# More squared tiles, an earlier norm chain and paired subtractions in a fused cross-covariance attention and highway layer

## The chip, the cores and the metric

The kernel runs on one NeuronCore of a Trainium2 chip. The metric is the time of one execution on the device, in microseconds. The engines are TensorE (PE, with its weight loads PEld), VectorE (DVE), ScalarE (ACT), GpSimd (POOL), and SyncE (SP), which only issues DMAs here.

## The reference

For each of four batches, q, k and v are 6336 x 256. The attention matrix is 256 x 256, a softmax over a product of columns that are normalized along the 6336 rows. Its output, all batches stacked to 25344 x 256, goes through a highway layer.

```python
qn = q / (np.linalg.norm(q, axis=1, keepdims=True) + 1e-06)
kn = k / (np.linalg.norm(k, axis=1, keepdims=True) + 1e-06)
s = kn.transpose(0, 2, 1) @ qn / tau
a = softmax(s)                       # along the last axis
x = (v @ a).reshape(B * S, D)
H = np.maximum(x @ w_h, 0.0)
T = 1.0 / (1.0 + np.exp(-(x @ w_t + b_t)))
out = T * H + (1.0 - T) * x
```

## The kernel before

The rows of a batch are 49 tiles of 128 and a last one of 64. Loads come from GpSimd's queue and turn f32 into f16. Two kinds of work run on PE.

*Scores.* For each tile, `emit_score` (L193) makes S += k^T q (two matmuls of 256 columns, L205) and the Gram blocks whose diagonals are the squared norms: two matmuls of 128 columns for k (L208), two for q (L214). For some runs of four tiles, the q Gram is replaced: ACT squares the tiles (L398), POOL adds halves (L404), DVE reduces the rest and the running sum into the next run's area (L411), and at the end two small f32 matmuls against ones (L457, "sums") add the column sums to the Gram. `decide` chooses such runs while it plans; there are 28 of them, none in batch 0.

*Slots.* Two tiles of v make a slot; there are 100, 25 in a batch. In each, PE transposes v (L236, "vtps"), DVE or ACT copies it out (L250, "vts"), and PE multiplies it by three 256 x 256 matrices that stand side by side in `mr`: a, a w_h and a w_t (L260, results x, h and zbank, four matmuls of 256 columns each). ACT fills zbank with the bias (L304) and makes T = sigmoid (tt, L301). DVE makes th = max(h, 0) T (L309) and ux = (T - 1) x (L317); POOL subtracts them, one slot at a time, into an out tile (L335), and SP stores four slots at once (L352). Two slots of zbank and four of th and ux are kept, seven out tiles (ORING), and three or more banks of PSUM for h and x.

*The chain.* Between the scores of a batch and its first slot stands `make_chain`. It takes the norms from the Gram diagonals (junk, L449; q first, then k), the root (ACT in batch 0, POOL's pow after, L475), adds 1e-6 and takes the reciprocal (L484, L490). The inverse norms of q are spread over all partitions by a matmul of a constant matrix with two diagonal matrices (dcat L494, cq L503). Then S is copied out (ssb, L464), multiplied by cq (L508), exponentiated (L519, in SBUF, with the inverse norms of k as scale), normalized into `mr` (L530, L533), transposed (at, L544; at_sb, L555) and multiplied by the highway's weights (ah, L563; copied at L574). Each of ACT's functions sqrt, exp and sigmoid needs another table, loaded at L435 or L519.

*The order.* A planner at the end of the kernel simulates the engines with given durations, and emits instructions in the order in which it would start them. Each engine has queues with a fixed order inside (chain, slots, transposes, scores on PE), and `step_pe`, `step_act`, `step_dve`, `step_pool` and `step_sp` say which one goes first. `slot_of_score` and S_END spread the scores of the next batch over the slots of this one, so that the chain of the next batch runs while slots of this one go on. Every engine then runs its list strictly in order. Stores are held back while loads queue; a held one is tied to the last subtraction that POOL had been given.

Of the kernel before, what the change touches and what calls it, by code (L numbers as in the profile page):

```python
# [60 lines left out]
def kernel(  # L61
# [38 lines left out]
    SQR, SQ_LATE = 4, 3  # L100
    CLOSE = 44
    DVE_SUBS, ACT_COPIES = 2, 77
    QRING, VRING, ORING = 4, 3, 7
    TTR, THR, VTR = 4, 4, 6
    OG = 4
    LASTS = list(range(16)) + [NPAIR - 1] + list(range(16, NPAIR - 1))
    PAIRS = [list(range(NPAIR))] * (B - 1) + [LASTS]
    S_END = [19, 44, 69]
# [15 lines left out]

    def nrows(i):
        return [P, REM] if i == NPAIR - 1 else [P, P]
# [6 lines left out]
    MM = lambda n: n / 2400.0 + 0.0025  # L133
# [59 lines left out]
    def emit_score(b, j):  # L193
        if j == 0:
            tags = ("S", "G") if b == 0 else ("hx1", "hx2")
            S_t[b] = psum_pool.tile([P, 2, C], f32, tag=tags[0], name=f"S{b}")
            G_t[b] = psum_pool.tile([P, 4, P], f32, tag=tags[1], name=f"G{b}")
        nr = REM if j == NS else P
        kk, qq = tile_of("k", b, j), tile_of("q", b, j)
        S, G = S_t[b], G_t[b]  # L200
        first, last = j == 0, j == NS
        gram_q = (b, j) not in squares
        for c in range(2):
            kc = kk[0:nr, bass.ts(c, P)]
            nc.tensor.matmul(  # L205
                S[:, c, :], kc, qq[0:nr, :], start=first and c == 0, stop=last and c == 1
            )
            nc.tensor.matmul(  # L208
                G[:, c, :], kc, kc, start=first and c == 0,
                stop=False, skip_group_check=True,  # L210
            )
        for c in range(2 if gram_q else 0):
            qc = qq[0:nr, bass.ts(c, P)]
            nc.tensor.matmul(  # L214
                G[:, 2 + c, :], qc, qc, start=False, stop=last and c == 1, skip_group_check=True
            )

    score = {}

    def make_score(b, j):  # L220
        t = Task(("S", b, j), "PE", 2 * MM(C) + 4 * MM(P), lambda e: emit_score(b, j))
        score[b, j] = t
        return t
# [67 lines left out]
    tts, ths, uxs, o_t, outs = {}, {}, {}, {}, {}  # L291
# [14 lines left out]
    def emit_th(t):  # L306
        ths[t] = work_pool.tile([P, 2, C], f32, tag="th", bufs=THR, name=f"th{t}")
        for pr, us in parts_of(t):
            nc.vector.scalar_tensor_tensor(  # L309
                out=ths[t][pr, us, :], in0=hx["h", t][pr, us, :], scalar=0.0,  # L310
                in1=tts[t][pr, us, :], op0=AluOp.max, op1=AluOp.mult,
            )

    def emit_ux(t):
        uxs[t] = work_pool.tile([P, 2, C], f32, tag="ux", bufs=THR, name=f"ux{t}")
        for pr, us in parts_of(t):
            nc.vector.scalar_tensor_tensor(  # L317
                out=uxs[t][pr, us, :], in0=tts[t][pr, us, :], scalar=1.0,
                in1=hx["x", t][pr, us, :], op0=AluOp.subtract, op1=AluOp.mult,
# [10 lines left out]
    def emit_sub(t, e):  # L330
        ot, o0 = out_tile(t)
        outs[t] = (ot, o0)
        sub = nc.vector if e == "DVE" else nc.gpsimd
        for pr, us in parts_of(t):
            ins = sub.tensor_tensor(  # L335
                out=ot[pr, o0 + us.start : o0 + us.stop, :], in0=ths[t][pr, us, :],
                in1=uxs[t][pr, us, :], op=AluOp.subtract,
# [25 lines left out]
    squares = set()  # L363
    runs = []
    areas = []
# [3 lines left out]
    def decide(b, j, now):  # L369
        if b == 0 or j == NS:  # L370
            return
        g = group_of(QG[b], j)
        g0, ns = QG[b][g]
        if j == CLOSE:
            mine = [r for r in runs if r.name[1] == b]
            if mine:
                chains[b]["sums"].after.append((mine[-1], TO_PE))
                sums_t[b] = len(runs) % SQR
        if g > 0 and j < CLOSE and (j - g0) % CH == 0 and g0 + ns - j >= CH:
            if sum(1 for r in runs if r.end is None) < SQ_LATE:  # L380
                squares.update((b, jj) for jj in range(j, j + CH))
                make_run(b, g, j)

    def make_run(b, g, j):
        n = len(runs)
        first = n == 0 or runs[-1].name[1] != b
        half = 1 if first else 2

        def area(m):
            if m % SQR == len(areas):  # L390
                areas.append(
                    work_pool.tile([P, CH + 1, C], f32, tag=f"sq{m}", bufs=1, name=f"sq{m}")
                )
            return areas[m % SQR]

        def square(e):
            o = j - QG[b][g][0]
            nc.scalar.activation(  # L398
                out=area(n)[:, 1:, :], in_=tiles["q", b, g][:, o : o + CH, :], func=Act.Square
# [17 lines left out]
        sq = Task(("sq", b, j), "ACT", 0.2 + CH * C / 1200.0, square)  # L417
        ad = Task(("add", b, j), "POOL", 0.1 + half * C * 0.00235, halves, [(sq, LAG)])
        rd = Task(("red", b, j), "DVE", 1.0, reduce, [(ad, LAG)])
        sq.after.append((task_of_load["q", b, g], LAND))  # L420
        if n >= SQR:
            sq.after.append((runs[n - SQR], LAG))
        if n >= 1:
            rd.after.append((runs[n - 1], LAG))
        runs.append(rd)
        if ("q", b, g) in recycler:
            recycler["q", b, g].after.append((sq, LAG + 0.2))
# [9 lines left out]
    def make_chain(b):  # L437
        st = {}
        T = {}
        last = score[b, NS]  # L440

# [13 lines left out]
        def pe_sums(e):  # L455
            for c in range(2 if b in sums_t else 0):
                nc.tensor.matmul(  # L457
                    G_t[b][:, 2 + c, :], areas[sums_t[b]][:, 0, bass.ts(c, P)], ones32,
                    start=False, stop=True, skip_group_check=True,
                )  # L460
# [5 lines left out]
        def root(kind):  # L466
            def emit(e):
                if "nrm" not in st:
                    st["nrm"] = work_pool.tile([P, 4], f32, tag="nrm", name=f"nrm{b}")
                o = 2 if kind == "q" else 0  # L470
                dst, src = st["nrm"][:, o : o + 2], st["n2"][:, o : o + 2]
# [8 lines left out]
        def invs(kind):  # L480
            def emit(e):
                o = 2 if kind == "q" else 0
                nrm = st["nrm"][:, o : o + 2]
                nc.vector.tensor_scalar(  # L484
                    out=nrm, in0=nrm, scalar1=1e-6, scalar2=None,
                    op0=AluOp.add, op1=AluOp.bypass,
                )
                if "inv" not in st:
                    st["inv"] = work_pool.tile([P, 4], f32, tag="inv", name=f"inv{b}")
                nc.vector.reciprocal(out=st["inv"][:, o : o + 2], in_=nrm)  # L490
                if kind == "q":
                    dcat = work_pool.tile([P, 2, P], f32, tag="dcat", bufs=1, name=f"dcat{b}")
                    for c in range(2):
                        nc.vector.tensor_scalar(  # L494
                            out=dcat[:, c, :], in0=ident0, scalar1=st["inv"][:, 2 + c : 3 + c],
                            scalar2=None, op0=AluOp.mult, op1=AluOp.bypass,
                        )
                    st["dcat"] = dcat
            return emit

        def pe_cq(e):
            cq = bank_tile(T["cq"], f"cq{b}")
            nc.tensor.matmul(cq[:, 0, :], taus, st["dcat"][:, :, :], start=True, stop=True)  # L503
# [10 lines left out]
        def exps(c):  # L514
            def emit(e):
                if c == 0:
                    st["rs"] = work_pool.tile([P, 2], f32, tag="rs", name=f"rs{b}")
                ar = st["ssb"]
                nc.scalar.activation(  # L519
                    out=ar[:, c, :], in_=ar[:, c, :], func=Act.Exp,  # L520
# [4 lines left out]
        def softmax(c):  # L525
            def emit(e):
                if c == 0:
# [6 lines left out]
                    out=mr_t[b][:, c, 0:C], in0=st["ssb"][:, c, :],  # L534
# [49 lines left out]
        after = [(last, PE_LAG)]  # L584
        if b > 0:
            add("sums", "PE", 0.5, pe_sums, [(score[b, CLOSE], 0.0)])
# [503 lines left out]
```

## Time and profile before

| | |
|---|---|
| median of 20 runs | 274.66 us (274.38 to 277.28) |
| the profiled execution, its own time | 274.74 us |
| its span, first to last instruction | 272.6 us |
| PE, DVE, ACT, POOL busy | 250.1, 207.1, 176.4, 203.7 us |
| matmuls | 2632 |
| TensorE clock granted | 0.996 of full |
| HBM read, written | 78.38, 25.95 MB |

Busy times are unions over the span. A matmul's duration in the trace contains its pipeline's latency; what counts for PE's pace is the distance of the starts. A row of the windows names a stretch of the span and the busy time of each engine in it, with the count of instructions in brackets.

### The profile page before, as it was taken

What the parts mean: (1) busy time and instruction counts of PE and PEld (TensorE: products, weight loads), DVE (VectorE), ACT (ScalarE), POOL (GpSimd) and SP (SyncE); (2) the same over time, 40 slices, a digit from 0 to 9 for tenths busy, and PEclk for the clock granted to TensorE, in tenths of its full rate; (3) what the DMA queues carried; (4) which work ended last, traced back from release to release, by engine and by line L of the source; (5) the groups of instructions that cost most, each with busy time, mean ns of one, the idle gap of its engine ahead of it and who ended that gap; (6) DMA issues with size and microseconds to landing.
All of it is one profiled execution on the core that took longest, in us unless ns stands there. A gap on an engine that the chain in (4) does not pass through costs nothing.

```text
span 272.6 us, 6603 instructions
## 1 busy us (share of the span) xinstructions
PE 250.1 (92%) x2632; PEld 217.4 (80%) x2632; DVE 207.1 (76%) x423; ACT 176.4 (65%) x292; POOL 203.7 (75%) x216
## 2 busy tenths in 40 slices
PE   0996897899999999999999999999999979999990
PEld 0686786788999886899999886999999847998780
DVE  2000036949989798899899798899999799999883
ACT  3310037858675478877575577968785788898880
POOL 5133463879999855998999857899998557988780
PEclk9999999999999999999999999999999999999998
DMA  7999999999999999999999999999999999793434
GB/s 211 213 215 213 204 204 222 214 209 217 216 208 214 219 213 291 250 299 288 275 299 243 219 227 284 264 299 297 271 258 253 353 408 266 173 338 159 185 126 182
DMA packets 16143, 66.08 MB, mean 242 GB/s; under 512 B 1777, under 2 KB 4338, under 8 KB 13170
## 3 DMA queue, kind: packets, MB, share of 16 engines
q0 software_dynamic: 11040, 38.67, 71.4%
q1 hardware_dynamic: 4786, 26.22, 24.3%
q10 hardware_dynamic: 288, 0.79, 0.7%
q8 instruction: 20, 0.33, 0.5%
q14 instruction: 9, 0.07, 0.1%
HBM read 78.38 MB, written 25.95 MB: 383 GB/s over the span
## 4 chain that ended last, share of the span: by engine, by line
PE 74%; DMA 12%; DVE 9%; issue 1%; POOL 1%; ACT 0%; DVEq 0%
PE zbank L260 14%; PE x L260 14%; PE h L260 14%; PE S L205 13%; DMA k<-in_k_dram 10%; PE vtps L236 7%; PE G L208 7%; PE G L214 2%; DVE th L309 2%; DMA qk<-in_k_dram 2%; DVE ux L317 2%; DVE mr L533 1%; DVE vts L250 1%; DVE nrm L484 1%; PE ah L563 1%
## 5 line engine op out<-in xcount | busy, mean ns | idle before, releaser
L335 POOL TENSOR_TENSOR o<-th,ux 128x512 f32<-128x512 f32 x94 | 120.3, 1292 | 24.5 <-DVE ux L317 22.8
L260 PEld LDWEIGHTS <-vts 128*128 128x128 f16 (+1 forms) x1200 | 111.2, 98 | 18.2 <-issue 6.2
L205 PE MATMUL S<-q,k 128*128 128x256 f16 x392 | 81.6, 278 | 10.6 <-ACT k L763 6.4
L301 ACT ACTIVATE tt<-zbank 128x512 f32<-128x512 f32 x100 | 59.7, 597 | 45.2 <-PE zbank L260 23.3
L309 DVE SCALAR_TENSOR_TENSOR th<-h,tt 128x512 f32<-128x512 f32 (+1 forms) x104 | 68.6, 663 | 12.0 <-ACT tt L301 9.0
L208 PE MATMUL G<-k 128*128 128x128 f16 x392 | 73.8, 222 | 0.0
L317 DVE SCALAR_TENSOR_TENSOR ux<-tt,x 128x512 f32<-128x512 f32 (+1 forms) x104 | 67.8, 655 | 0.0
L260 PE MATMUL x<-mr,vts 128*128 128x256 f16 (+1 forms) x400 | 60.5, 273 | 0.7 <-DVE th L309 0.7
L260 PE MATMUL zbank<-mr,vts 128*128 128x256 f16 (+1 forms) x400 | 60.5, 273 | 0.0
L260 PE MATMUL h<-mr,vts 128*128 128x256 f16 (+1 forms) x400 | 60.5, 273 | 0.0
L304 ACT COPY zbank<-btb 128x512 f32<-128x512 f32 x98 | 57.8, 591 | 2.9
L205 PEld LDWEIGHTS <-k 128*128 128x128 f16 x392 | 39.0, 100 | 15.9 <-ACT k L763 6.4
L208 PEld LDWEIGHTS <-k 128*128 128x128 f16 x392 | 39.1, 100 | 1.2 <-issue 0.3
L236 PE MATMUL vtps<-ident,v 128*128 128x128 f16 x392 | 38.2, 219 | 1.7 <-DVE vts L250 1.4
L250 DVE COPY vts<-vtps 128x512 f16<-128x512 f16 x82 | 34.3, 418 | 6.4 <-PE vtps L236 5.4
L404 POOL TENSOR_TENSOR sq<-sq 128x512 f32<-128x512 f32 (+1 forms) x28 | 33.9, 1213 | 3.2 <-ACT sq L398 3.2
L236 PEld LDWEIGHTS <-v 128*128 128x128 f16 x392 | 28.0, 98 | 5.0 <-issue 2.8
L155 POOL DMA_DIRECT2D q<-in_q_dram x25 | 14.0, 561 | 23.9 <-PE G L214 21.3
L449 DVE SCALAR_TENSOR_TENSOR junk<-G,ident 128x128 f32<-128x128 f32 x16 | 4.7, 291 | 33.5 <-PE G L214 33.1
L411 DVE TENSOR_REDUCE sq<-sq 128x256 f32<-128x768 f32 x28 | 28.7, 1026 | 1.6 <-POOL sq L404 1.6
L398 ACT ACTIVATE sq<-q 128x1024 f32<-128x1024 f16 x28 | 29.2, 1054 | 0.0
L214 PE MATMUL G<-q 128*128 128x128 f16 x168 | 24.0, 226 | 0.0
(67 smaller groups left out, 143.1 us busy)
## 6 DMA issues: line engine op xcount, KB each, us to landing
out_dram<-o SPq DMA_DIRECT2D x23, 1024.0 KB, 8.9
v<-in_v_dram POOLq DMA_DIRECT2D x11, 768.0 KB, 17.9
q<-in_q_dram POOLq DMA_DIRECT2D x7, 768.0 KB, 18.8
k<-in_k_dram POOLq DMA_DIRECT2D x7, 768.0 KB, 20.8
q<-in_q_dram POOLq DMA_DIRECT2D x9, 512.0 KB, 13.5
k<-in_k_dram POOLq DMA_DIRECT2D x9, 512.0 KB, 14.6
v<-in_v_dram POOLq DMA_DIRECT2D x4, 832.0 KB, 19.2
q<-in_q_dram POOLq DMA_DIRECT2D x4, 256.0 KB, 12.8
```

The lines of the kernel that those rows point to most:

```text
L205: nc.tensor.matmul(S[:, c, :], kc, qq[0:nr, :], start=first and c == 0, stop=last and c == 1)
L208: nc.tensor.matmul(G[:, c, :], kc, kc, start=first and c == 0, stop=False, skip_group_check=True,)
L214: nc.tensor.matmul(G[:, 2 + c, :], qc, qc, start=False, stop=last and c == 1, skip_group_check=True)
L236: nc.tensor.transpose(ps[:, u, c, 0:r], vt[0:r, bass.ts(c, P)], ident[0:r, 0:r])
L250: cp(out=sb, in_=ps)
L260: nc.tensor.matmul(dst[0:r, u, :], vT_t[t][:, u, kt, 0:r], mr[:, kt, off : off + C], start=(not seeded and kt == 0 and (u == 0 or i == NPA ...
L301: nc.scalar.activation(out=tts[t], in_=zbank[t % 2], func=Act.Sigmoid)
L304: nc.scalar.copy(out=zbank[t % 2], in_=btb)
L309: nc.vector.scalar_tensor_tensor(out=ths[t][pr, us, :], in0=hx["h", t][pr, us, :], scalar=0.0, in1=tts[t][pr, us, :], op0=AluOp.max, op1=A ...
L317: nc.vector.scalar_tensor_tensor(out=uxs[t][pr, us, :], in0=tts[t][pr, us, :], scalar=1.0, in1=hx["x", t][pr, us, :], op0=AluOp.subtract, ...
L335: ins = sub.tensor_tensor(out=ot[pr, o0 + us.start : o0 + us.stop, :], in0=ths[t][pr, us, :], in1=uxs[t][pr, us, :], op=AluOp.subtract,)
L404: nc.gpsimd.tensor_tensor(out=sq[:, 1 : 1 + half, :], in0=sq[:, 1 : 1 + half, :], in1=sq[:, 1 + CH - half : 1 + CH, :], op=AluOp.add,)
```

## The change

- The runs of squared tiles are a fixed list (RUNS): 22 of q and 17 of k in batches 1 to 3, 39 in all. Each kind has areas of its own, four for q and two for k.
- The last tiles of each batch (TAIL: 6, 12, 10, 7) are taken apart: all their q Grams, then their k Grams, then their S. The 64-row tile goes ahead of them. The norms wait only for the Grams.
- The subtraction is done in place: th is written into the out tile and ux subtracted from it, for two slots in one instruction of 128 x 1024. The last eight slots are done singly, the subtraction of slot 97 is split between POOL and DVE.
- 1e-6 is not added: a constant column of the tile nrm holds it, and a reduction over two columns adds it to the root. cq is made by two matmuls, each with the inverse norm repeated over 128 columns as weights and the identity over tau as moving operand; dcat is gone.
- Exp writes to PSUM where a bank is to be had (both halves in batches 0 and 3, the first half in batches 1 and 2). Its table is loaded ahead by an instruction of its own, and no sigmoid is planned between it and the load of the sigmoid table.
- 28 copies of vts at fixed slots go to ACT (14 before). Numbers of the planner change: S_END, when loads of q, k and v are due (QOFF, VOFF), how far PE runs ahead (SAHEAD, LOOKS), and how many finished groups stores are held back (HOLD).

```diff
-    SQR, SQ_LATE = 4, 3
+    SQR = {"q": 4, "k": 2}
+    RUNS = {1: {'q': [4, 8, 20, 32, 36, 44], 'k': [0, 8, 24, 28, 32, 40]}, 2: {'q': [0, 8, 12, 16, 20, 24, 28, 36, 40], 'k': [0, 12, 16, 32, 40]}, 3: {'q': [8, 12, 20, 28, 32, 40, 44], 'k': [0, 8, 16, 28, 32, 36]}}
+    TAIL = [6, 12, 10, 7]
+    QOFF, VOFF = [1.5, 3.0, 4.0, 0.5], [7.5, 3.5, 0.5, 9.5]
+    SAHEAD = [0, 0.5, 10.0, 10.5]
+    HOLD = [2, 1, 1, 5]
...
-    TTR, THR, VTR = 4, 4, 6
+    TTR, UXR, VTR = 4, 3, 5
...
-    S_END = [19, 44, 69]
+    S_END = [21.5, 42.5, 65.0]
...
+        order = list(range(NS - tail)) + [NS] + list(range(NS - tail, NS))
+        steps = [(j, "skq") for j in order[: NS + 1 - tail]]
+        for parts in "qks":
+            steps += [(j, parts) for j in order[NS + 1 - tail :]]
...
-                out=ths[t][pr, us, :], in0=hx["h", t][pr, us, :], scalar=0.0,
-                in1=tts[t][pr, us, :], op0=AluOp.max, op1=AluOp.mult,
+                out=ot[pr, o0 + us.start : o0 + us.stop, :], in0=hx["h", t][pr, us, :],
+                scalar=0.0, in1=tts[t][pr, us, :], op0=AluOp.max, op1=AluOp.mult,
...
+            dst = ot[pr, o0 + us.start : o0 + us.stop, :]
             ins = sub.tensor_tensor(
-                out=ot[pr, o0 + us.start : o0 + us.stop, :], in0=ths[t][pr, us, :],
-                in1=uxs[t][pr, us, :], op=AluOp.subtract,
+                out=dst, in0=dst, in1=uxs[n][pr, us, :], op=AluOp.subtract
             )
...
-                nc.vector.tensor_scalar(
-                    out=nrm, in0=nrm, scalar1=1e-6, scalar2=None,
-                    op0=AluOp.add, op1=AluOp.bypass,
-                )
...
+                nc.vector.tensor_reduce(
+                    out=inv, in_=nrm[:, o : o + 2, :], axis=mybir.AxisListType.X, op=AluOp.add
+                )
+                nc.vector.reciprocal(out=inv, in_=inv)
...
-            nc.tensor.matmul(cq[:, 0, :], taus, st["dcat"][:, :, :], start=True, stop=True)
+            for c in range(2):
+                nc.tensor.matmul(
+                    cq[:, 0, bass.ts(c, P)],
+                    st["inv"][:, 2 + c : 3 + c].to_broadcast([P, P]), ident_tau,
+                    start=(c == 0), stop=(c == 1),
+                )
...
+                if c == 0:
+                    st["e", c] = st["cq"][:, 1, :]
+                elif T["exps", 1].bank is not None:
+                    st["e", c] = bank_tile(T["exps", 1], f"e{b}")[:, 0, :]
+                else:
+                    st["e", c] = ar[:, c, :]
                 nc.scalar.activation(
-                    out=ar[:, c, :], in_=ar[:, c, :], func=Act.Exp,
+                    out=st["e", c], in_=ar[:, c, :], func=Act.Exp,
...
+        add("table", "ACT", 1.5, lambda e: preload_table(Act.Exp),
+            [(T["root", "k"], 0.0)] if b == 0 else [(T["invs", "q"], EXP_LAG)])
...
-                    SUB[t].after.append((s.dma, LAG))
+                    TH[t].after.append((s.dma, LAG))
...
-        if dma.backlog(0) + dma.backlog(1) > 3.0 and ready_groups < ORING - 2 and not late:
+        if dma.backlog(0) + dma.backlog(1) > 3.0 and ready_groups < ORING - HOLD[min(slot_now() // NPAIR, B - 1)] and not late:
             return False
```

## The prediction

> **What bounds the kernel now.** I read the page first, then the windows of 10 us, the groups with shapes kept apart, the timelines of each engine around the three softmax chains, and the DMA issues with their landings.
>
> The page:
>
> ```profile
> PE 250.1 (92%) x2632; PEld 217.4 (80%) x2632; DVE 207.1 (76%) x423; ACT 176.4 (65%) x292; POOL 203.7 (75%) x216
> ...
> PE   0996897899999999999999999999999979999990
> ...
> DVE  2000036949989798899899798899999799999883
> ...
> POOL 5133463879999855998999857899998557988780
> ...
> DMA  7999999999999999999999999999999999793434
> ```
>
> From about 60 us on PE is full, but DVE and POOL stand at 9 tenths beside it and the DMA engines are full to about 230 us. So it is PE's time, with little air on three sides. The windows say where PE is less than full:
>
> ```profile
> 140.00:150.00 10.00, 10.00 (x115) 9.25 (x113) 9.60 (x17) 5.79 (x10) 9.84 (x11) 1.00 1.07 265
> ...
> 160.00:170.00 10.00, 10.00 (x100) 7.50 (x98) 8.57 (x22) 8.59 (x16) 7.44 (x8) 1.00 1.04 266
> ...
> 220.00:230.00 10.00, 8.33 (x71) 5.67 (x70) 9.48 (x22) 7.63 (x16) 6.15 (x7) 1.00 1.02 310
> 230.00:240.00 10.00, 10.00 (x108) 9.11 (x106) 9.60 (x18) 9.18 (x17) 8.95 (x9) 1.00 0.85 215
> ```
>
> (The columns are PE, PEld, DVE, ACT, POOL, clock, DMA, GB/s.) 71 matmuls where the next window holds 108: this is the chain of batch 3, which ends just before its first slot. By the ends of the x matmuls, slots 19 to 24, 44 to 49 and 69 to 74 take 15.6, 15.1 and 12.6 us. Their matmuls, at 109 ns for 256 columns and 55 ns for 128 (the starts in PE's timeline), are 13.7, 13.7 and 9.1 us, and 0.6 more goes to the 64-row tile's slot in each. So the chains cost 1.3, 0.8 and 2.9 us: 5.0 in all. Why the chains are long:
>
> ```profile
> 94.46 1.36 DVE L484 TENSOR_SCALAR nrm<-nrm 128x2 f32<-128x2 f32 x1
> ...
> 101.56 1.48 DVE L533 TENSOR_SCALAR mr<-ssb,rinv 128x256 f16<-128x256 f32 x1
> ...
> 103.15 0.36 DVE L533 TENSOR_SCALAR mr<-ssb,rinv 128x256 f16<-128x256 f32 x1
> ...
> 94.50 1.29 POOL L335 TENSOR_TENSOR o<-th,ux 128x512 f32<-128x512 f32 x1
> ...
> 100.34 2.55 POOL L335 TENSOR_TENSOR o<-th,ux 128x512 f32<-128x512 f32 x2 [1.23 <-DVE ux L317]
> ```
>
> The same instruction takes 0.36 us alone and 1.48 beside a subtraction on POOL; the tiny one 0.16 and 1.36.
>
> **The change, part by part.** All sums are against the profiled execution: 274.74 us, its span 272.6 and 2.1 around it; the median of the runs is 274.66.
>
> *Matmuls.* Squared tiles go from 28 runs to 39, and now of k too. Each run of 4 tiles spares 8 Gram matmuls: 11 x 8 = 88. Their price and that of the column sums put in:
>
> ```profile
> 206.70 0.27 PE L214 MATMUL G<-q 128*128 128x128 f16 x2
> 206.81 0.60 PE L260 MATMUL zbank<-mr,vts 128*128 128x256 f16 x4
> ...
> 211.42 0.66 PE L457 MATMUL G<-ones,sq 128*128 128x128 f32 x4
> ```
>
> Two take 0.11 us, so 88 x 0.055 = 4.8 us less. The sums of k need two more f32 products per batch; two took 0.60 (211.42 to the next matmul at 212.02), so 3 x 0.6 = 1.8 more. Net -3.0. [...]
>
> *Start.* Loads of batch 0 set it: the last land at 34.8 us and PE then works off 6 us of matmuls. Late tiles' Grams before their S let the first norms start about 1.3 us earlier (6 tiles of two 256-column S matmuls, 6 x 0.218). But the copy of S still waits for the last S and stands before the k root and the exp table. I take 0.8 us for the chain; then k of batch 1 (landed 52.9, used at 52.95) and v (landed 56.8, used 57.6) hold the PE as before. So -0.5, bounds -0.8 and 0.
>
> *The chains.* What goes: the add of 1e-6 (two of eight took 1.34 and more, the others 0.16), the two dcat products (2 x 0.24 a chain), the softmax's SBUF source (two of eight at 1.44 and more). What comes: a sum over two numbers in place of the add, c_q from two f32 products in place of one of double width (0.53 us, as many columns), exp into PSUM, the exp table loaded while the logits are made. The count of table loads stays 10 (1.28 us each). [...] The row for a 128x256 cast from PSUM is 0.41 us, against 0.36: 8 x 0.05 = 0.4 dearer over all chains, against two waits of 1.1. [...] In batches 1 and 2 the second half still lies in SBUF, and a subtraction beside it is now longer (below): bounds of each such wait 0 and 2.4. Where it counts more: S of batches 1 to 3 now ends near slots 21, 42 and 64 instead of 18, 43 and 68, so chain 3 has ten slots (15 us at 1.53 us) before its first use; the chain of batch 1 took 15.1 us from the last S (92.1) to the copied weights (107.2). And PE has 13 score tiles of batch 2 after slot 22 and 9 of batch 3 after slot 45 to fill the other two. Of chain 3's 2.9 us I take 2.2 back, of the other 2.1 us 0.8: -3.0 (bounds -5.0 and 0).
>
> *POOL.* 88 subtractions become 44 of 128x1024. 128x256 costs 0.72 us and 128x512 1.28 (starts back to back), so 1024 is about 2.40: 44 x (2.56 - 2.40) = -7.0. 11 more halves: 11 x 1.24 = +13.6. POOL has 6.6 us more, not less.
>
> *DVE.* 11 more reductions at 0.95 (their pitch): +10.4. 14 copies move to ACT: 14 x 0.34 = -4.8. The chains give some 5 back. About even in sum, but PE asks sooner: in slots 9 to 74 DVE has 143.5 us of work, PE 147.1.
>
> *ACT.* 11 squares x 0.99 and 14 copies x 0.51: +18 us on 176, in a span of 272. Hidden, save around the tables, when no sigmoid may run (about 4 us; zbank is two deep, about two slots of 2.2).
>
> *th now written into the out tile.* It costs the same, but the wait for the out ring's store moves from POOL's subtraction to DVE's th, and behind a waiting th stand ux, the vts copies and the reductions; PE waits for them through three hx banks. Stores are also held back about four slots longer than before, which gives the loads the DMA engines. 7 out tiles; the tightest is the first of batch 1: its store is tied to the subtraction of slot 49, its tile is needed by th of slot 54, some 3.5 slots x 2.1 = 7.4 us later. Stores took
>
> ```profile
> DMA to landing us min/median/max: 2.0/6.8/15.1
> ```
>
> and about 10 us in that stage (o25: 159.76 to 170.72). Cost between 0 and 7.7; 10 - 7.4 = 2.6 on DVE; as k3_2 and this store compete, I take 1.
>
> *Closer engines.* Cutting slots 9 to 74 into stretches of eight slots and taking the busiest engine's work in each (counts by pitch) gives 153.4 us before and 153.0 after; the actual was 157.8. So of the 3.0 us saved on PE some is not free: with POOL the busiest in many stretches I take +1.0 beside the 1 for the store; bounds 0 and 2.6.
>
> Loads: the last q and k land at 202.6 and are used at 206.4; only 4 us of air, but held-back stores make about 2 MB (5 us) of room. I take 0. The last 25 slots stay at 1.53 us each; the end with its split subtraction, 0.
>
> Sum: -0.5 - 3.0 - 3.0 + 1.0 + 1.0 = -4.5: **270.2 us**.
>
> **The rivals.** *All waits go* (B): start -0.8, matmuls -3.0, chains -5.0: 265.9. For it: PE's filler stands exactly in the chains. Against: DVE at 9.6 already.
> *The side engines hold the pace* (C): the stretch sums differ by 0.4, the chain stalls come back as waits for POOL and DVE, start -0.5: 273.8, that is, no or hardly any change. For it: POOL's +6.6 us and its 9.5 to 10 us of 10 at 60 to 90 and 130 to 150 us. Against: POOL runs three pairs behind without hurting anybody.
> *The out ring stalls DVE* (D, slower): one place, th of slot 54. It eats the whole 4.5 us when that store takes over 7.4 + 1 + 4.5 = 12.9 us to land; one of the stores before took 15.06 because another was issued 1.6 us ahead, and here two are tied to slot 49. At 15.1 the time is 270.2 - 1 + 7.7 = 276.9.
> That PE doesn't get the matmuls off its path is C.
>
> **How the numbers follow.** A 0.50 (270.2, by itself 268 to 272.5), B 0.18, C 0.18, D 0.14. A measurement of this kernel tells about 0.2% (0.5 us) from no change. C straddles this: a third of it each faster, same and slower. Faster 0.5 + 0.18 + 0.06 + a little of D that is under 12 us = 0.76, same 0.07, slower 0.17. The range for 8 in 10 takes in most of B and all of C: 265.8 to 275.0.
>
> **What would show it.** Right: PE's matmul count down by about 80; DVE's mr from PSUM at 0.4 us with no 1.4 among batches 0 and 3; the window at the turn to batch 3 (slots 70 to 76) with 105 matmuls or more per 10 us; POOL pairs near 2.4 us. Wrong: th waiting on an out store near slot 54; PE waiting on DVE's copies or POOL's on ux in slots 25 to 40; PE waiting for k in slots 23, 46 or for v at slot 68, where the loads now come as late as PE.

## The result, and the profile after

The changed kernel takes 271.18 us (median of 7 runs, 270.36 to 275.32), the kernel before 274.74 (48 runs): a ratio of 0.985 [0.983, 0.988], 3.6 us less. Forecast were 270.2 us and a range of 265.8 to 275.0. The slowest of the seven, 275.32, counts as a slow run and is left out of the ratio. The profiled execution took 270.91 us, its span 269.1 (before 272.6).

The page of the changed kernel (busy times and slices, then the chain that ended last):

```profile
PE 246.5 (92%) x2564; PEld 214.0 (80%) x2564; DVE 207.2 (77%) x414; ACT 192.6 (72%) x320; POOL 206.4 (77%) x183
...
PE   0996887899999999999999989999999999999990
...
DVE  2000035869999999899999789899999998999894
...
POOL 6133455499989999999899988898966486977880
...
DMA  7999999999999999999999999999999999699435
...
PE 52%; DMA 29%; POOL 8%; DVE 5%; issue 2%; ACT 1%; DVEq 0%; POOLq 0%; ACTq 0%
DMA k<-in_k_dram 24%; PE x L317 11%; PE h L317 10%; PE zbank L317 10%; PE S L230 8%; PE vtps L293 5%; POOL o L399 3%; DMA out_dram<-o 3%; PE G L234 3%; PE G L239 3%; DMA qk<-in_k_dram 2%; DVE o L366 1%; DVE ux L376 1%; POOL q L177 1%; POOL sqq L454 1%
```

PE has 68 matmuls fewer and is 3.6 us less busy; DVE's time is that of before, ACT's is 16 us more and POOL's 2.7. The rows of tenths look alike. What differs is the chain, here with loads of k at 24%. The same line of the kernel before:

```profile
PE zbank L260 14%; PE x L260 14%; PE h L260 14%; PE S L205 13%; DMA k<-in_k_dram 10%; PE vtps L236 7%; PE G L208 7%; PE G L214 2%; DVE th L309 2%; DMA qk<-in_k_dram 2%; DVE ux L317 2%; DVE mr L533 1%; DVE vts L250 1%; DVE nrm L484 1%; PE ah L563 1%
```

There they were 10%. The time no longer hangs on PE alone.

The windows of the changed kernel (PE, PEld, DVE, ACT, POOL, clock, DMA, GB/s):

```profile
140.00:150.00 10.00, 9.86 (x105) 8.87 (x103) 9.05 (x15) 7.45 (x13) 10.00 (x11) 1.00 1.05 310
150.00:160.00 10.00, 8.89 (x97) 7.84 (x96) 7.71 (x27) 7.11 (x14) 9.23 (x9) 1.00 1.06 225
160.00:170.00 10.00, 10.00 (x100) 7.71 (x98) 9.20 (x19) 9.16 (x16) 8.35 (x9) 1.00 1.04 220
...
220.00:230.00 10.00, 10.00 (x100) 8.05 (x99) 8.99 (x20) 7.51 (x14) 7.22 (x5) 1.00 0.98 401
```

The hole at 220 to 230 us is gone, 100 matmuls where there were 71. But 140 to 150 holds 105 (before 115), and 150 to 160 is a new hole.

To see this by slots, take the time from the end of one slot's x matmuls to that of another, and out of it the lost time: every distance between two matmul starts that is more than 0.1 us over the matmul's own pitch (by the starts in PE's timeline 109 ns for 256 columns, where a single one is listed with 0.27 us, 55 for 128, and twice that for f32 products, whose starts lie 0.11 us apart for 128 columns), summed without that pitch. In us:

| slots | before: time, lost | after: time, lost |
|---|---|---|
| 4 to 19 | 36.8, 0.8 | 34.0, 0.2 |
| 19 to 24 (chain 1) | 15.6, 1.2 | 17.7, 0 |
| 24 to 44 | 45.0, 0 | 43.6, 1.2 |
| 44 to 49 (chain 2) | 15.1, 0.6 | 18.0, 1.4 |
| 49 to 64 | 31.9, 0 | 33.8, 0.8 |
| 64 to 74 (chain 3) | 25.3, 2.6 | 19.7, 1.5 |
| 74 to 79 | 7.8, 0 | 7.8, 0 |
| sum | 177.6, 5.2 | 174.7, 5.1 |

(The times also differ because the score tiles lie in other slots.) Slot 4 ends 0.2 us earlier than before, slots 79 to 99 take 31.4 us in both, and what follows slot 99 is 0.3 shorter. So 2.9 of the 3.5 us of span are here, and nearly all of that is matmuls that are not there (their pitches add up to 168.5 us before and 165.9 after): the lost time is as large as before. It lies elsewhere, which is what the experiments are about. The waits of the changed kernel name the candidates (us in total, times, longest):

```profile
PEld L230 <- DMA k<-in_k_dram: 6.9, 5, 2.3
...
ACT sqk L448 <- DMA k<-in_k_dram: 4.3, 3, 2.8
...
PE x L317 <- DVE o L366: 1.4, 2, 0.8
DVE o L366 <- DMA out_dram<-o: 1.2, 1, 1.2
```

The longest of these, in ACT's timeline (start, duration, in brackets the idle time before it and what ended that):

```profile
149.65 0.58 ACT L307 COPY vts<-vtps 128x512 f16<-128x512 f16 x1
153.01 1.06 ACT L448 ACTIVATE sqk<-k 128x1024 f32<-128x1024 f16 x1 [2.78 <-DMA k<-in_k_dram]
153.97 0.58 ACT L358 ACTIVATE tt<-zbank 128x512 f32<-128x512 f32 x1
```

in DVE's, with the wait for the store some 28 us later:

```profile
154.58 0.69 DVE L366 SCALAR_TENSOR_TENSOR o<-h,tt 128x512 f32<-128x512 f32 x1 [1.68 <-ACT tt L358]
155.19 0.68 DVE L376 SCALAR_TENSOR_TENSOR ux<-tt,x 128x512 f32<-128x512 f32 x1
155.79 0.15 DVE L539 TENSOR_REDUCE inv<-nrm 128x2 f32<-128x4 f32 x1
...
182.28 0.69 DVE L366 SCALAR_TENSOR_TENSOR o<-h,tt 128x512 f32<-128x512 f32 x1 [1.22 <-DMA out_dram<-o]
```

and in PE's:

```profile
155.33 0.60 PE L317 MATMUL x<-mr,vts 128*128 128x256 f16 x4 [0.75 <-DVE o L366]
156.28 0.68 PE L548 MATMUL cq<-ident_tau,inv 128*128 128x128 f32 x4 [0.35 <-DVE inv L542]
...
183.02 0.60 PE L317 MATMUL x<-mr,vts 128*128 128x256 f16 x4 [0.66 <-DVE o L366]
```

Read from the top: a group of k of batch 3 landed at 152.93. ACT was to square it and had been idle for 2.78 us; behind the square stood a sigmoid, which needed nothing from that load. DVE's th waited 1.68 us for this sigmoid, PE 0.75 for th, and the inverse norms of chain 2 stood behind th. One late load went through three queues, and PE's own wait doesn't name it. The second is the store that the prediction had priced: it landed at 182.18 after 9.29 us, th waited 1.2 and PE 0.7.

### The profile page after: what moved, and what is told of

It reads as the page before. It is cut to its first block, busy times and chain, and to the rows that moved or that the text cites. A ratio compares the mean times of both kernels' runs of the same rounds, so it can differ in the third digit from the quotient of the medians.

```text
span 269.1 us, 6452 instructions
## 1 busy us (share of the span) xinstructions
PE 246.5 (92%) x2564; PEld 214.0 (80%) x2564; DVE 207.2 (77%) x414; ACT 192.6 (72%) x320; POOL 206.4 (77%) x183
## 3 DMA queue, kind: packets, MB, share of 16 engines
HBM read 78.38 MB, written 25.95 MB: 388 GB/s over the span
## 4 chain that ended last, share of the span: by engine, by line
PE 52%; DMA 29%; POOL 8%; DVE 5%; issue 2%; ACT 1%; DVEq 0%; POOLq 0%; ACTq 0%
DMA k<-in_k_dram 24%; PE x L317 11%; PE h L317 10%; PE zbank L317 10%; PE S L230 8%; PE vtps L293 5%; POOL o L399 3%; DMA out_dram<-o 3%; PE G L234 3%; PE G L239 3%; DMA qk<-in_k_dram 2%; DVE o L366 1%; DVE ux L376 1%; POOL q L177 1%; POOL sqq L454 1%
## 5 line engine op out<-in xcount | busy, mean ns | idle before, releaser
L399 POOL TENSOR_TENSOR o<-o,ux 128x1024 f32<-128x1024 f32 (+2 forms) x50 | 111.3, 2231 | 23.0 <-DVE ux L376 19.1
L317 PEld LDWEIGHTS <-vts 128*128 128x128 f16 x1200 | 111.7, 98 | 17.5 <-issue 5.5
L230 PE MATMUL S<-q,k 128*128 128x256 f16 x392 | 73.7, 278 | 12.1 <-ACT k L834 6.3
L366 DVE SCALAR_TENSOR_TENSOR o<-h,tt 128x512 f32<-128x512 f32 x96 | 65.6, 683 | 7.7 <-ACT tt L358 4.7
L230 PEld LDWEIGHTS <-k 128*128 128x128 f16 x392 | 37.7, 100 | 18.3 <-DMA k<-in_k_dram 6.9
L234 PE MATMUL G<-k 128*128 128x128 f16 x256 | 44.1, 224 | 0.7 <-DVE junk L502 0.7
L307 DVE COPY vts<-vtps 128x512 f16<-128x512 f16 x68 | 28.6, 420 | 6.5 <-PE vtps L293 6.0
L454 POOL TENSOR_TENSOR sqq<-sqq 128x512 f32<-128x512 f32 (+1 forms) x22 | 26.4, 1204 | 0.1
L234 PEld LDWEIGHTS <-k 128*128 128x128 f16 x256 | 24.0, 101 | 1.8 <-issue 1.1
L448 ACT ACTIVATE sqq<-q 128x1024 f32<-128x1024 f16 x22 | 23.0, 1055 | 0.1
L461 DVE TENSOR_REDUCE sqq<-sqq 128x256 f32<-128x768 f32 x22 | 22.6, 1026 | 0.0
```

The lines of the kernel that those rows point to most:

```text
L230: nc.tensor.matmul(S[:, c, :], kc, qq[0:nr, :], start=first and c == 0, stop=last and c == 1)
L234: nc.tensor.matmul(G[:, c, :], kc, kc, start=begins(b), stop=False, skip_group_check=True,)
L307: cp(out=sb, in_=ps)
L317: nc.tensor.matmul(dst[0:r, u, :], vT_t[t][:, u, kt, 0:r], mr[:, kt, off : off + C], start=(not seeded and kt == 0 and (u == 0 or i == NPA ...
L366: nc.vector.scalar_tensor_tensor(out=ot[pr, o0 + us.start : o0 + us.stop, :], in0=hx["h", t][pr, us, :], scalar=0.0, in1=tts[t][pr, us, :] ...
L399: ins = sub.tensor_tensor(out=dst, in0=dst, in1=uxs[n][pr, us, :], op=AluOp.subtract)
```

## The experiments

The theory at the outset was the prediction's: PE sets the time, and the side engines give back about 1 us. Its rivals: the transfers do, or POOL does. All runs are compared with the same kernel before (274.6 to 274.8); "after" is the changed kernel. Edits of instructions that leave the rest in place keep the order of the changed kernel; where an edit gives the planner other numbers, the whole order is planned anew, and then part of a difference can be due to that.

| kernel | median, us | ratio to before |
|---|---|---|
| after | 271.18 | 0.985 [0.983, 0.988] |
| Grams put back | 272.96 | 0.994 [0.992, 0.996] |
| after, few stores | 268.13 | 0.977 [0.974, 0.979] |
| before, few stores | 274.64 | 1.000 [0.998, 1.002] |
| few stores and Grams put back | 272.28 | 0.990 [0.988, 0.992] |
| exp to SBUF | 273.79 | 0.995 [0.993, 0.997] |
| q runs only (planned anew) | 276.96 | 1.008 [1.006, 1.010] |
| single subtractions (anew) | 280.51 | 1.022 [1.017, 1.027] |
| S ends of before (anew) | 277.05 | 1.008 [1.007, 1.010] |
| S ends of after on before (anew) | 277.72 | 1.011 [1.008, 1.014] |
| load and store times of before (anew) | 275.14 | 1.002 [1.000, 1.003] |
| no late Grams first (anew) | 277.61 | 1.009 [1.007, 1.011] |
| two loads of v later (anew) | 272.10 | 0.990 [0.987, 0.994] |

**1. What are the spared matmuls worth?**

```diff
+                if ("k", b, j) in squares and j // CH * CH in BACK[b]:
+                    nc.tensor.matmul(
+                        G[:, c, :], kc, kc, start=begins(b), stop=False, skip_group_check=True,
+                    )
...
+    BACK = {1: [0, 8, 24, 28], 2: [0, 12, 16, 32], 3: [0, 8, 16]}
```

> The order of the changed kernel, with the 88 Gram matmuls of 11 runs of k put back where their score tiles stand, the squares kept as well (so these tiles' k norms count double; the sums are only larger). Theory PE: the spared matmuls are the gain, so they cost 88 x 0.055 = 4.8 us when they return; +3.5 to +4.8 us over the changed kernel's 271.2, that is 274.7 to 276. Rival side engines: PE waits for POOL, DVE or loads anyway and takes the matmuls into those waits; +0 to +1.5 us.

272.96 us: 1.8 more by the medians, 2.4 by the ratios (1.6 to 3.2, from the two intervals), 3.2 by the profiled spans. Not all of 4.8, and not nothing. Of the 88, 72 lie between slots 4 and 79; the others are before slot 4, where the loads of the start set the pace. 72 x 0.055 = 4.0. In the profiled execution the lost time between those slots is 3.8 instead of 5.1: PE spends 1.3 us of the additional matmuls where it would have waited. That execution (274.36 us) is the slowest of the seven, so the usual share spent in waits is rather larger: of the 4.0 us only 1.8 show in the medians.

**2. Who makes it wait? Few stores.** In both kernels, of each group of eight output tiles in batches 0 to 2 only the first is stored; the rest of the output is left out, 16.5 MB of 25.95.

```diff
-        parts = [(rows(ob)[:, 2 * i0 : 2 * (i0 + n), :], ot[:, o0 : o0 + 2 * n, :])]
+        parts = [(rows(ob)[:, 2 * i0 : 2 * (i0 + n) if b == B - 1 else 2 * i0 + 1, :], ot[:, o0 : o0 + 2 * n if b == B - 1 else o0 + 1, :])]
```

> The changed kernel in the same order, but of each group of four slots of batches 0 to 2 only the first of eight tiles is stored (the rest of these outputs is left out): 16.5 MB less through the DMA engines from 91 us on. Theory DMA: what the changed kernel lost again in slots 24 to 66 are loads and one out tile that come late, so -1.5 to -3 us (268 to 269.7). Rival side engines: POOL and DVE set the pace there, within 0.5 us of 271.2.

> The kernel before with the same part of the stores left out. Its loads land 4 to 14 us ahead of their use after 80 us, so both theories expect no more than 0.5 us from 274.7; if it is 1.5 us faster or more, the DMA engines slowed even the kernel before, through more than late loads.

The changed kernel gains 3.0 us, the kernel before nothing (0.1, within the noise). Up to slot 24 the changed kernel stays as it was, then it is ahead by 0.8 at slot 29, 1.3 at 44, 2.2 at 49 and 3.0 at 59, and keeps that to the end. Its lost time falls from 5.1 to 2.2. The page and ACT's timeline of the changed kernel with few stores:

```profile
DMA  7999999999999999999992999999353611599435
```

```profile
149.32 1.06 ACT L448 ACTIVATE sqk<-k 128x1024 f32<-128x1024 f16 x1
150.28 0.59 ACT L358 ACTIVATE tt<-zbank 128x512 f32<-128x512 f32 x1
```

The square that had waited for its load until 153.01 starts at 149.32 without a wait: its k now lands at 139.81. The DMA engines have holes where they had none. Yet the row of the kernel before was full as well, and taking the same stores from it changed nothing. The difference is the air between a load's landing and its first use: the third group of k of batch 2 landed at 101.45 and was used at 111.3 before, in the changed kernel at 104.96 and 105.00; the second of batch 3 at 151.75 and 160.0, now at 152.93 and 153.01. The landings moved by 1 to 3.5 us, the uses by 6 to 7: score tiles are worked off earlier, to end S of batches 2 and 3 by slots 42 and 64, and their squares earlier still.

**3. Both edits together.** The edits are those of 1 and 2.

> The changed kernel with both edits at once: the 88 Gram matmuls of the eleven k runs put back, and of each group of eight output tiles in batches 0 to 2 only the first stored (the rest of the output stays out; the norms of those k tiles count double). The order of all other instructions is that of the changed kernel. The question is who swallowed a part of the 4.8 us when the matmuls alone were put back (272.96 against 271.18). If it was the transfers, that is, PE had waited for late k tiles anyhow, then here PE has to carry all of it: 268.13 + 4.8 = 272.9. If it was POOL and DVE, which stand as close without the stores, the difference stays at about 1.8: 269.9. Between 271 and 272 both have a share.

272.28 us: 4.2 more by the medians than with few stores alone, 3.7 by the ratios, 3.9 by the spans, and the lost time is 1.9 against 2.2. With loads in time, PE pays for all of the 72 matmuls, 3.9 us or 54 ns each. So in 1 it was the transfers that took their share, not POOL or DVE. The medians of 1 and 3 alone lie far enough apart for that, the ratios hardly; the lost times carry it. The windows of this kernel at the place of the hole:

```profile
140.00:150.00 10.00, 10.00 (x114) 9.20 (x113) 9.55 (x15) 7.39 (x14) 10.00 (x9) 1.00 0.46 93
150.00:160.00 10.00, 10.00 (x113) 9.33 (x111) 9.27 (x30) 9.42 (x17) 9.41 (x11) 1.00 1.04 214
```

PE is full with 114 and 113 matmuls, beside a POOL that is busy for 10.00 and 9.41 us: a full POOL did not hold PE here.

**4. The runs of k.**

```diff
-'k': [0, 8, 24, 28, 32, 40]}, 2: ... 'k': [0, 12, 16, 32, 40]}, 3: ... 'k': [0, 8, 16, 28, 32, 36]}
+'k': []}, 2: ... 'k': []}, 3: ... 'k': []}
```

> The changed kernel without its 17 runs of k (22 runs of q remain), planned anew: 136 Gram matmuls of k back, 17 squares, halvings and reductions and the three sums of k away. For PE 136 x 0.055 - 1.8 = 5.7 us more, for POOL about 17 x 1.24 = 21 us less, for DVE 17 us less, for ACT 17 us less. If PE alone sets the pace: 271.2 + 5.7 = 276.9. If POOL and DVE set it in the stretches where runs lie, it is no slower than the changed kernel, down to 268. Between 273 and 275 both have a share, as the run with the Grams put back suggests.

276.96 us, 5.8 more: PE's sum (5.7) to the tenth, though the whole was planned anew. The page:

```profile
PE 250.5 (91%) x2688; PEld 218.9 (80%) x2688; DVE 192.5 (70%) x397; ACT 177.0 (64%) x303; POOL 187.4 (68%) x166
```

The lost time is 4.8 us against 5.1, but it lies elsewhere (2.0 of it is one wait for v at 169 us), so that the agreement to the tenth is partly chance. 19 us less for POOL, 15 for DVE and 16 for ACT bought nothing. The runs of k alone are worth more than the whole difference between the kernels.

**5. The paired subtractions.**

```diff
-    SINGLES = 8
+    SINGLES = 100
```

> The changed kernel planned anew with every subtraction for one slot alone: POOL gets 44 x (2 x 1.28 - 2.37) = 8.4 us more. Theory POOL among the bounds: +1 to +3 us. Rival: POOL has slack over three pairs of ux, and single subtractions finish sooner; -0.5 to +0.5 us.

280.51 us, 9.3 more, for 44 x (2 x 1.28 - 2.37) = 8.4 us more work on POOL: far outside of both expectations. Lost time is 16.5 us, 11.4 more than in the changed kernel. The two longest waits of PE, 3.2 and 2.7 us beyond the pitch, go back to loads of k; ACT's and PE's timelines:

```profile
143.14 1.06 ACT L448 ACTIVATE sqk<-k 128x1024 f32<-128x1024 f16 x1 [4.41 <-DMA k<-in_k_dram]
...
144.72 0.58 PE L293 MATMUL vtps<-ident,v 128*128 128x128 f16 x4 [3.08 <-ACT vts L307]
...
168.66 0.40 PE L230 MATMUL S<-q,k 128*128 128x256 f16 x1 [2.51 <-DMA k<-in_k_dram]
```

After each of them the granted clock is at half for 3.4 us (0.63 and 0.52 in the windows 144 to 146 and 146 to 148), which costs 1.6 and 1.5 us more: 9.0 of the 16.5. The first of these loads landed no later than in the changed kernel (143.03 against 144.15); the new order has its square three slots earlier, in slot 38. The second was issued at 155.19 instead of 145.33. Another 4.0 us are waits for DVE and ACT in slot 25. So the kernel without pairs loses more than the whole gain, but that POOL's additional work is the cause is not shown: most of what can be traced are loads and the order planned anew.

**6. Exp into PSUM.**

```diff
-                    st["e", c] = st["cq"][:, 1, :]
+                    st["e", c] = ar[:, c, :]
...
-                    st["e", c] = bank_tile(T["exps", 1], f"e{b}")[:, 0, :]
+                    st["e", c] = ar[:, c, :]
```

> The order of the changed kernel, with both halves of exp written to SBUF as before, in all four batches (the bank is reserved all the same). Theory contention: six softmax products, now SBUF to SBUF, stand beside paired subtractions of 2.37 us and wait 0 to 2.3 us each; with two or three hit, +0.5 to +2 us. Rival: the chains have air now (batch 3's by slots, the others' by filler), and the product is cheaper by 0.1 us: -0.2 to +0.3 us.

273.79 us: 2.6 more by the medians, 1.6 in the profiled execution, which is the fastest of its runs; 1.4 of the 1.6 come between slots 64 and 69. DVE's timeline there, of the changed kernel:

```profile
208.97 0.48 DVE L588 TENSOR_SCALAR mr<-cq,rinv 128x256 f16<-128x256 f32 x1
209.37 0.15 DVE L585 RECIPROCAL rinv<-rs 128x1 f32<-128x1 f32 x1
209.56 0.48 DVE L588 TENSOR_SCALAR mr<-e,rinv 128x256 f16<-128x256 f32 x1
```

and of the one with exp in SBUF:

```profile
209.11 2.02 DVE L588 TENSOR_SCALAR mr<-ssb,rinv 128x256 f16<-128x256 f32 x1
211.05 0.15 DVE L585 RECIPROCAL rinv<-rs 128x1 f32<-128x1 f32 x1
211.24 0.35 DVE L588 TENSOR_SCALAR mr<-ssb,rinv 128x256 f16<-128x256 f32 x1
```

with POOL's timeline of the same execution:

```profile
208.64 2.33 POOL L399 TENSOR_TENSOR o<-o,ux 128x1024 f32<-128x1024 f32 x1 [0.72 <-DVE ux L376]
```

and PE's:

```profile
211.18 0.28 PE L599 MATMUL at<-ident,mr 128*128 128x128 f16 x2 [1.11 <-DVE mr L588]
```

The instruction that takes 0.35 us alone starts while the pair runs (208.64 to 210.97) and ends 0.16 us after it. From PSUM it is 0.48 each time, also beside the same pair (208.50 to 210.85 in the changed kernel). Before, with subtractions of 1.29 us on POOL, it took 1.48 at most; beside the pair of 2.33 us it takes 2.02 here.

**7. Where S ends.** On the changed kernel the ends of before, on the kernel before the new ends:

```diff
-    S_END = [21.5, 42.5, 65.0]
+    S_END = [19, 44, 69]
```

> The changed kernel planned anew with the ends of the scores of before (slots 19, 44, 69 instead of 21.5, 42.5, 65; S of batch 3 then ends after slot 68). Theory chain placement: batch 3's chain stalls PE again at its first slot, 2 to 4 us over 271.2. Rival: the shorter chain (no add, no dcat, table loaded ahead, Grams first) hides the end anyway; within 0.7 us, or faster, as loads are due later.

```diff
-    S_END = [19, 44, 69]
+    S_END = [21.5, 42.5, 65.0]
```

> The kernel before with only the ends of the scores moved to 21.5, 42.5 and 65. Theory chain placement: its worst stall (2.9 us at slots 69 to 74) goes, -2 to -3 us from 274.7. Rival: with its 28 runs and old loads it hasn't the room to finish the scores of batch 3 four slots earlier and gives it back there; within 0.7 us.

277.05 (5.9 more than after) and 277.72 (3.0 more than before, 2.0 in the profiled execution), both outside of what was expected. Neither the new ends alone nor the rest without them gains anything. On the kernel before, slots 64 to 74 lose 3.0 us with the new ends and 2.6 with the old, so chain 3 gains nothing by its earlier place alone, and slots 19 to 29 and 44 to 49 lose 2.9 more. With the old ends on the changed kernel slots 69 to 74 take 15.7 us instead of 8.2, lost 5.6. Its windows:

```profile
210.00:220.00 10.00, 8.08 (x82) 7.11 (x81) 9.25 (x28) 7.59 (x15) 6.03 (x4) 1.00 1.00 348
220.00:230.00 10.00, 8.18 (x56) 5.21 (x56) 7.09 (x15) 6.36 (x12) 3.10 (x2) 0.83 0.56 233
```

Chain 3 with nothing left to fill PE: worse than before the change, 56 matmuls, and a granted clock of 0.83 in that window.

**8. When loads and stores are due.**

```diff
-    QOFF, VOFF = [1.5, 3.0, 4.0, 0.5], [7.5, 3.5, 0.5, 9.5]
+    QOFF, VOFF = [3.0, 3.0, 3.0, 3.0], [5.0, 5.0, 5.0, 5.0]
...
-    HOLD = [2, 1, 1, 5]
+    HOLD = [2, 2, 2, 2]
```

> The changed kernel planned anew with the due times of loads and the holding back of stores as before (3.0 and 5.0 slots, two groups). Theory DMA: the stores take their share earlier, k of batches 2 and 3 comes later and PE waits for it; 1 to 3 us over 271.2. Rival: the one store that DVE waits for is earlier, which is worth its 1 us; -1 to 0 us.

275.14 us, 4.0 more, no better than the kernel before. The waits:

```profile
PEld L230 <- DMA k<-in_k_dram: 10.3, 7, 2.6
```

3.4 us more of them than in the changed kernel. The longest is that for the third group of k of batch 3; all others lie before slot 4, which ends only 0.2 us later than in the changed kernel. PE's timeline:

```profile
164.71 0.28 PE L230 MATMUL S<-q,k 128*128 128x256 f16 x1 [2.46 <-DMA k<-in_k_dram]
```

In the changed kernel this group landed at 160.20 and was used at 162.01. The order of the transfers is a condition of the gain; this agrees with 2, though the whole plan is another one here too.

**9. Late tiles' Grams first.**

```diff
-    TAIL = [6, 12, 10, 7]
+    TAIL = [0, 0, 0, 0]
```

> The changed kernel with each tile's Grams beside its scores to the last tile, as in the kernel before (no late tiles' Grams first), planned anew; the work is the same. The prediction took 0.5 us at the start from this step and a part of the chains' 3.0: the first norms come some 1.3 us later in each batch. By it: slots 0 to 20 later by 0.5 to 0.8, and each chain up to 1.3 longer, of which a part shows: 272 to 274. Rival: the copy of S, the root table and the exp table follow the last S anyhow, so that nothing is lost: 271.2.

277.61 us, 6.4 more: outside of both expectations. At the start nothing is lost (slot 4 ends 0.3 us later than in the changed kernel, slot 19 0.1 earlier), though the weights of batch 0 come at 47.7 us instead of 45.6: PE waits for loads anyhow. 4.4 us come by slot 29, 1.2 more between 64 and 69. DVE's timeline of this kernel:

```profile
103.40 1.02 DVE L461 TENSOR_REDUCE sqk<-sqk 128x256 f32<-128x768 f32 x1
104.61 0.29 DVE L502 SCALAR_TENSOR_TENSOR junk<-G,ident 128x128 f32<-128x128 f32 x1 [0.19 <-PE G L511]
...
107.11 0.14 DVE L539 TENSOR_REDUCE inv<-nrm 128x2 f32<-128x4 f32 x1
```

The last S of batch 1 is done at 93.8 us here; the reductions of its runs come at 102.1 and 103.4, and only then the sums and the norms, which in the changed kernel were extracted at 95.1, before the last S (96.4). The weights are ready 21.0 us after S instead of 11.7. PE waits three times between 100.7 and 103.2 us, and after that the granted clock is at half from 104.0 to 107.4 us, which accounts for about 1.6 of the 4.4 us (a row of the windows):

```profile
104.00:106.00 2.00, 2.00 (x14) 1.62 (x13) 1.71 (x10) 2.00 (x3) 2.00 (x4) 0.50 1.06 219
```

How much of the rest is the tail and how much the new plan, which put those reductions behind five slots' th and ux, this run can't tell.

**10. Could the loads be put in a better order?**

```diff
-    QOFF, VOFF = [1.5, 3.0, 4.0, 0.5], [7.5, 3.5, 0.5, 9.5]
+    QOFF, VOFF = [1.5, 3.0, 4.0, 0.5], [7.5, 2.5, 0.5, 4.0]
```

> The changed kernel with two loads moved in the queue and nothing else in the loads: the second group of v of batch 1 behind the fourth group of q and k of batch 2 (it landed 8.9 us before its use, while that k tile came 0.7 us late at 116.7), and the last group of v of batch 2 before the first of batch 3 (1.6 us of air against 20.6); planned anew. If the lateness of single loads can be mended by their order, 0.7 us in slots 25 to 30 come back and little else changes: 270.5. If the DMA engines are simply full there, the wait moves to the next load: 271.2. Since the order of the engines is planned anew, 1 us either way can come from that.

272.10 us, 0.9 more by the medians, 1.4 by the ratios, 0.7 by the spans. Slots 24 to 29 lose nothing any more (0.7 in the changed kernel) and 44 to 49 0.7 instead of 1.4, but 19 to 24 lose 0.6 instead of 0 and 39 to 44 1.9 instead of 0.4. The waits moved to other places. No kernel with the whole output was faster than the changed one.

## Why the prediction was right

It named 270.2 us and the time is 271.2; the direction, and the case held likeliest, were right. Against its own steps, by the spans and the lost times:

| step | predicted | measured | |
|---|---|---|---|
| start | -0.5 | -0.2 | end of slot 4 |
| matmuls | -3.0 | -2.9 | slots 4 to 79, time less lost time |
| chains and closer side engines | -3.0 + 1.0 = -2.0 | -3.0 | lost time, before to few stores: 5.2 to 2.2 |
| th waits for its store | +1.0 | +0.8 | slots 54 to 59, gone with few stores |
| loads | 0 | +2.1 | the rest of what few stores take off the lost time, 5.1 to 2.2 |
| end | 0 | -0.3 | after slot 99 |
| sum | -4.5 | -3.5 | spans: -3.5 |

*Matmuls.* Right in size and in kind, by the row of 55 ns: the 72 of experiment 3 cost 3.9 us, 54 ns each. Experiment 4 agrees with PE's arithmetic for 136 of them. The net came out better than its parts: the 16 of the 88 that lie before slot 4 gained little (0.2 us at the end of slot 4, with all that changed there), and the additional f32 products of the sums cost 0.11 us each, 1.3 in all and not 1.8, since the 0.60 us that were read for four of them contain about 0.15 of waiting.

*Chains.* Chain 3 gave 1.1 of the 2.2 us taken: the hole before slot 74 is gone, but slots 64 to 69 lose 1.5 where they lost nothing, since the chain lies there now. Chain 1 gave all of its 1.2. Chain 2 gave nothing even with few stores (0.6 us lost, as before), and in the kernel as it is 1.4 us are lost there to the late k of batch 3 (ACT's square at 153.01); so the two gave 0.4 of the 0.8 taken. The last 0.6 of the 3.0 are in slots 4 to 19, for which the prediction had nothing. The softmax from PSUM costs 0.484 us, not 0.41: eight halves would be 8 x 0.13 = 1.0 dearer than the 0.353 from SBUF, six of them in PSUM 0.8. By these two times alone this step would be a loss. Experiment 6 says a gain of 1.6 to 2.6 us, of which the one wait seen in its trace, in chain 3, explains 1.4; the prediction had set two waits of 1.1 against 0.4.

*POOL and closer engines.* The groups of the changed kernel (busy in total, mean ns, idle before):

```profile
L399 POOL TENSOR_TENSOR o<-o,ux 128x1024 f32<-128x1024 f32 x44 | 104.2, 2369 | 22.4 <-DVE ux L376 18.6 <-issue 2.5 <-DVE inv L539 0.6
...
L454 POOL TENSOR_TENSOR sqq<-sqq 128x512 f32<-128x512 f32 x19 | 24.2, 1276 | 0.1
...
L461 DVE TENSOR_REDUCE sqq<-sqq 128x256 f32<-128x768 f32 x22 | 22.6, 1026 | 0.0
L448 ACT ACTIVATE sqk<-k 128x1024 f32<-128x1024 f16 x17 | 17.9, 1054 | 4.3 <-DMA k<-in_k_dram 4.3
```

2369 ns for the pair, where 2.40 us had been worked out, against 1292 for a subtraction of one slot in the same view of before (taken as 1.28): the 88 subtractions became 44 x (2 x 1.292 - 2.369) = 9.5 us cheaper instead of 7.0. The adds grew by 12.6 us instead of 13.6, as three of the new ones are short. POOL's busy time rose by 2.7 us in place of 6.6. That the side engines give back 1 us was not found: experiments 3 and 4 show no price of their being close. What the pairs are worth to the whole stays open, since experiment 5 mixes them with late loads and another order.

*Out ring.* Place, size and victim were right: a store of 9.29 us (estimated 10), 1.2 us of th (1.0), at slot 54. The slower rival needed 12.9. That was close: the two stores were issued 0.4 us apart, and the second took 16.24.

*Loads.* This is the step that failed. The prediction says: "only 4 us of air, but held-back stores make about 2 MB (5 us) of room. I take 0." The air was read where it was before. The change uses k of batches 2 and 3 six to seven microseconds earlier, which the new ends say outright (four slots of about 2 us for batch 3), and air of 4 to 14 us minus 7 leaves late loads wherever a stream is full. The step on ACT failed with it: that its 18 us more are hidden is true for the work, but the squares of k stand in ACT's one queue, ahead of sigmoids, and wait there for loads that PE would want only later. The loads cost 2.1 us that were put at nothing; chains and side engines together gave 1.0 more than was taken. That the one made up for half of the other is luck: the total is better than its terms.

The rivals: that all waits go (265.9) would have needed the transfers out of the way; with few stores it was 268.1. That the side engines hold the pace (273.8) is refuted by experiments 3 and 4 for this kernel; for one without pairs, 5 leaves it open. Of the signs named, the 105 matmuls per 10 us at the turn to batch 3 were set too high: PE is full there with 100.

## What to carry to other kernels

When a change lets the bounding engine ask for its inputs earlier, subtract the shift from the air of each load before taking the loads as hidden: here the full DMA rows before and after look alike, and only the distance from landing to first use (101.45 to 111.3 us before, 104.96 to 105.00 after, for the third group of k of batch 2) told which kernel is bound by them. An instruction that waits for a load early in one engine's strict queue stalls what stands behind it, and the wait then shows under another name on the critical engine: here a square on ACT waited 2.78 us, th on DVE 1.68 behind it, and PE 0.75 for th. Parts of such a change are no independent gains: of five that were undone (runs of k, pairs, late Grams, S ends, load times), each left a kernel slower than, or no faster than, the one before, though a part of that lies in the plans that were made anew.

## What the runs showed of the hardware that was not expected

A long PE stall had a second price. In the changed kernel with the old ends of S, PE ran only six matmuls from 217.6 to 222.8 us while chain 3 was made. PE's timeline just after:

```profile
222.85 0.58 PE L293 MATMUL vtps<-ident,v 128*128 128x128 f16 x4 [1.48 <-ACT vts L307]
223.22 1.06 PE L317 MATMUL zbank<-mr,vts 128*128 128x256 f16 x4
224.08 1.06 PE L317 MATMUL h<-mr,vts 128*128 128x256 f16 x4
224.93 1.06 PE L317 MATMUL x<-mr,vts 128*128 128x256 f16 x4
...
226.28 0.61 PE L317 MATMUL zbank<-mr,vts 128*128 128x256 f16 x4
```

Four matmuls of 256 columns take 0.86 us from start to start instead of 0.44, for three groups; the granted clock was 0.50 from 222.62 to 226.03 us and 1.00 on either side. That is 3 x 0.42 = 1.3 us on top of the stall.

The half clock was measured behind shorter waits too: ahead of the half clock from 104.0 us in experiment 9, PE waited three times between 100.7 and 103.2 us, and the longest idle time listed there is 0.58 us. Up to slot 99 the profiled executions of this case have seven such stretches behind the first rise of the clock, each 3.41 us long: this one, one each in experiments 8 and 10 (from 43.3 and 44.0 us, where loads set the pace), and two each in 5 (144.5 and 168.4) and 9 (42.6 and 104.0). In the kernels before and after the clock stays at 1.00 from that rise to slot 99, also where the kernel before starts only 7 matmuls from 222 to 224 us. So a part of the loss in experiments 5, 7 and 9 is this clock. What brings it on was not shown.
